# Decode attention over a 32,768-key cache: two more score columns on VectorE, a pipelined end, and longer rows for the output projection

## The chip, the cores and the metric

The kernel runs on one core of one Trainium2 chip. The metric is the device time of one execution in microseconds (us). PE is the matmul engine, VectorE (DVE) and ScalarE (ACT) the two elementwise engines, SP the engine that issues the loads, PEld PE's loading of weights. The granted clock is the share of PE's full speed that the trace records.

## The reference

One token attends over 32 heads of 32,768 keys of 192 numbers, then goes through a small two-layer network. All data is bf16. What matters here:

```python
q = (layernorm(x) @ wq).reshape(32, 192)             # x: 640, wq: 640 x 6144
p = softmax((q · k_cache) * 192**-0.5)               # k_cache: 32 x 32768 x 192, 403 MB
o = p · v_cache                                      # v_cache: the same size
h = x + o.reshape(6144) @ wo                         # wo: 6144 x 640
out = h + relu(layernorm(h) @ w1) @ w2               # w1: 640 x 1536, w2: 1536 x 640
```

K and V are read once and used for one query: 805 MB of the 825 MB that the kernel loads.

## The kernel before

A head's keys come in loads of 64 columns (8192 keys, 128 partitions x 24,576 B, 3 MiB), K and V alternately, from one queue into three buffers each. A load is worked in two chunks of 32 columns. Of a chunk, 12 columns are scored on VectorE (multiply by the query, reduce) and 20 on PE, which must first transpose them in 30 blocks of 128 x 128, copied out of PSUM by ScalarE. The exponentials, and their sums, are ScalarE's; then PE multiplies the probabilities with V. The last load of all is cut into 40, 16 and 8 columns.

```python
full = [(JL, [(J, 20), (J, 20)])] * (Sk // (P * JL))          # J = 32 columns, 20 of them on PE
ends = full[:-1] + [(40, [(20, 12), (20, 12)]), (16, [(16, 10)]), (8, [(8, 4)])]
# ... (cut)
wo_view = A_wo.rearrange("(b p) n -> p b n", p=P)             # rows of 1280 B
# ... (cut)
def o_scale(h):
    # ... (cut)
    nc.vector.tensor_scalar_mul(out=dst[:, 0, n0:n0 + Dh], in0=o[:, 0:Dh], scalar1=s[0:2, 1:2])
    nc.scalar.activation(out=dst[:, 1, n0:n0 + Dh], in_=o[:, Dh:2 * Dh], func=F.Copy, scale=s[0:2, 1:2])
# ... (cut)
for g in range(G):                      # chunks of all heads
    # ... loads of this chunk (cut)
    transposes(g)
    if g > 0:
        pv(g - 1)                       # probabilities times V, one chunk behind
    scores_pe(g)
    sc = scores_dve(g)
    # ... once per head: denominator, scaling, turning, projection, next query (cut)
    exp_dve(g, sc)
den_mm(H - 1); den_rec(H - 1); pv(G - 1); o_scale(H - 1); o_turn(H - 1); project(H // 2 - 1)
# ... second layernorm and the two layers (cut)
```

The softmax here doesn't subtract the row's maximum and nothing guards it: scores larger than these inputs give would overflow.

Of the kernel before, what the change touches and what calls it, by code (L numbers as in the profile page):

```python
# [9 lines left out]
F = mybir.ActivationFunctionType  # L10
# [3 lines left out]
def kernel(  # L14
# [12 lines left out]
    nc = tc.nc  # L27
    P = nc.NUM_PARTITIONS

    Bsz, Sq, D = A_x.shape  # L30
    _, H, Sk, Dh = A_k_cache.shape
# [9 lines left out]
    JL = 64  # L41
    J = 32
# [2 lines left out]



    full = [(JL, [(J, 20), (J, 20)])] * (Sk // (P * JL))
    ends = full[:-1] + [(40, [(20, 12), (20, 12)]), (16, [(16, 10)]), (8, [(8, 4)])]
    NEND = 3  # L50
    loads = []
    chunks = []
    for h in range(H):
        k0 = c = 0
# [8 lines left out]
            k0 += P * jl  # L63
        assert k0 == Sk
    G = len(chunks)
    NCH = [sum(1 for q in chunks if q[0] == h) for h in range(H)]
    NCM = max(NCH)
    NBM = max(q[5] for q in chunks) * Dh // P
# [3 lines left out]
    kpool = ctx.enter_context(tc.tile_pool(name="kpool", bufs=3))  # L72
    vpool = ctx.enter_context(tc.tile_pool(name="vpool", bufs=3))
# [3 lines left out]
    tsb = ctx.enter_context(tc.tile_pool(name="tsb", bufs=2))  # L77
    prp = ctx.enter_context(tc.tile_pool(name="prp", bufs=1))
    scp = ctx.enter_context(tc.tile_pool(name="scp", bufs=3))
    pcp = ctx.enter_context(tc.tile_pool(name="pcp", bufs=3))  # L80
    small = ctx.enter_context(tc.tile_pool(name="small", bufs=2))
    tps = ctx.enter_context(tc.tile_pool(name="tps", bufs=3, space=bass.MemoryType.PSUM))
    sps = ctx.enter_context(tc.tile_pool(name="sps", bufs=1, space=bass.MemoryType.PSUM))
# [4 lines left out]
    def mm_bank(shape, dtype, name):  # L88
        return mps.tile(shape, dtype, tag="mm", name=name)

    k_hd = A_k_cache.rearrange("b h s d -> (b h) s d")
    v_hd = A_v_cache.rearrange("b h s d -> (b h) s d")
    wq_view = A_wq.rearrange("(c p) n -> p c n", p=P)
    wo_view = A_wo.rearrange("(b p) n -> p b n", p=P)


    x_row = const.tile([DT, P], bf16)
# [5 lines left out]
    vt_t = {}  # L103
# [6 lines left out]

    def load_wo(pr):
        t = wop.tile([P, 3, D], bf16, name="wo")
        nc.sync.dma_start(out=t[:], in_=wo_view[:, 3 * pr:3 * pr + 3, :])
        wo_t[pr] = t

    def load_part(ld, src, pool, tag, name):
        h, k0, jl = loads[ld]
        if ld == len(loads) - 1:
            pool, tag, size = wqp, "wq", DT * QG * Dh
        else:  # L120
            size = JL * Dh
        t = pool.tile([P, size], bf16, tag=tag, name=name)
        nc.sync.dma_start(out=t[:, 0:jl * Dh], in_=src[h, k0:k0 + P * jl, :].rearrange("(p j) d -> p (j d)", p=P))
        return t

    def load_k(ld):
        kt_t[ld] = load_part(ld, k_hd, kpool, "kt", "kt")

    def load_v(ld):
        vt_t[ld] = load_part(ld, v_hd, vpool, "vt", "vt")  # L130

    w_t = {}

    def load_w(name, src, pool, tag, pieces):
        n, N = src.shape[0] // P, src.shape[1]
        assert n * N <= JL * Dh and n % pieces == 0
        t = pool.tile([P, JL * Dh], bf16, tag=tag, name=tag)
        v = t[:, 0:n * N].rearrange("p (c n) -> p c n", n=N)
        for i in range(pieces):
            c0, c1 = i * n // pieces, (i + 1) * n // pieces  # L140
            nc.sync.dma_start(out=v[:, c0:c1], in_=src.rearrange("(c p) n -> p c n", p=P)[:, c0:c1])
        for c in range(n):
            w_t[name, c] = v[:, c, :]
# [21 lines left out]
    o_pair = [const.tile([2, 2, 2 * Dh], f32, name=f"o_pair{i}") for i in range(2)]  # L165
# [25 lines left out]
    with tc.manual_schedule():  # L191
# [37 lines left out]
        def transposes(g):  # L229
            h, c, ld, c0, jc, jp = chunks[g]  # L230
            kt = kt_t[ld]
            NB = jp * Dh // P
            kT = tsb.tile([P, NBM, P], bf16, name="kT")
            for b0 in range(0, NB, 8):
                nb = min(8, NB - b0)
                tp = tps.tile([P, 8, P], bf16, name="tp")
                for b in range(nb):
                    off = (c0 + jc - jp) * Dh + (b0 + b) * P
                    nc.tensor.transpose(out=tp[:, b, :], in_=kt[:, off:off + P], identity=ident_b[:])  # L239
                nc.scalar.copy(out=kT[:, b0:b0 + nb, :], in_=tp[:, 0:nb, :])  # L240
            kT_t[g] = kT
# [18 lines left out]
        def scores_dve(g):  # L260
            h, c, ld, c0, jc, jp = chunks[g]
            kt = kt_t[ld]
            JD = jc - jp
            qb = qb_t[h]
            pr = prp.tile([P, JDM, Dh], f32, name="pr")
            nc.vector.tensor_tensor(out=pr[:, 0:JD, :], in0=kt[:, c0 * Dh:(c0 + JD) * Dh].rearrange("p (j d) -> p j d", d=Dh),  # L266
                                    in1=qb[:].unsqueeze(1).to_broadcast([P, JD, Dh]), op=A.mult)
            sc = scp.tile([P, J], f32, name="sc")
            nc.vector.reduce_sum(out=sc[:, 0:JD], in_=pr[:, 0:JD, :], axis=mybir.AxisListType.X)  # L269
            return sc  # L270

        def exp_dve(g, sc):
            h, c, ld, c0, jc, jp = chunks[g]
            JD = jc - jp
            pA = pcp.tile([P, J], bf16, name="pA")
            nc.scalar.activation(out=pA[:, 0:JD], in_=sc[:, 0:JD], func=F.Exp, scale=SCALE,  # L276
                                 accum_out=dsums[:, h, 2 * c:2 * c + 1])
            pA_t[g] = pA

        def pv(g):  # L280

            h, c, ld, c0, jc, jp = chunks[g]
            JD = jc - jp
            vt, pA, pB = vt_t[ld], pA_t.pop(g), pB_t.pop(g)
            if c == 0:
                o_t[h] = ops.tile([2, 2 * Dh], f32, name="o_ps")
            o = o_t[h]
            order = list(range(JD, jc, 2)) + list(range(0, JD, 2))
            for i, j in enumerate(order):
                p = pA[:, j:j + 2] if j < JD else pB[:, j - JD:j - JD + 2]  # L290
                first = c == 0 and i == 0
                last = c == NCH[h] - 1 and i == len(order) - 1
                nc.tensor.matmul(o[:], lhsT=p, rhs=vt[:, (c0 + j) * Dh:(c0 + j + 2) * Dh], start=first, stop=last)  # L293
# [3 lines left out]
        def den_mm(h):  # L297
            d = mm_bank([P, 2 * NCM], f32, "den")
            nc.tensor.matmul(d[:], lhsT=ones_mat[:], rhs=dsums[:, h, :], start=True, stop=True)  # L299
            den_t[h] = d  # L300

        def den_rec(h):
            d = den_t.pop(h)
            s = small.tile([P, 2], f32, tag="rec", name="rec")
            nc.vector.reduce_sum(out=s[:, 0:1], in_=d[:], axis=mybir.AxisListType.X)  # L305
            nc.vector.reciprocal(out=s[:, 1:2], in_=s[:, 0:1])
            den_t[h] = s

        def o_scale(h):
            s = den_t.pop(h)  # L310
            o = o_t.pop(h)
            dst = o_pair[(h // 2) % 2]
            n0 = (h % 2) * Dh
            nc.vector.tensor_scalar_mul(out=dst[:, 0, n0:n0 + Dh], in0=o[:, 0:Dh], scalar1=s[0:2, 1:2])  # L314
            nc.scalar.activation(out=dst[:, 1, n0:n0 + Dh], in_=o[:, Dh:2 * Dh], func=F.Copy, scale=s[0:2, 1:2])  # L315

        oT_t = {}

# [21 lines left out]

        load_k(0)
        load_v(0)
        q_rows(0)
        q_spread(0)
        for g in range(G):
            h, c, ld, c0, jc, jp = chunks[g]
            end = ld - (len(loads) - NEND)
            if end == 0 and c0 == 0:
                for i in range(NEND):
                    load_k(ld + i)  # L350
                for i in range(NEND):
                    load_v(ld + i)

                load_w("w1", B_w1, kpool, "kt", 1)
                load_w("w2", B_w2, vpool, "vt", 2)
            elif end < 0 and c0 == 0 and g > 0:
                load_k(ld)
                load_v(ld)
            if c == 1 and h % 2 == 0:
                load_wo(h // 2)  # L360
            if c == 3 and h % QG == QG - 2 and h + 2 < H:
                load_wq(h // QG + 1)
            transposes(g)
            if g > 0:
                pv(g - 1)
            scores_pe(g)
            sc = scores_dve(g)
            if c == 0 and h > 0:
                den_mm(h - 1)
                den_rec(h - 1)  # L370
                o_scale(h - 1)
            if c == 1 and h > 0:
                o_turn(h - 1)
            if c == 2 and h > 0 and h % 2 == 0:
                project(h // 2 - 1)
            if c == 4 and h + 1 < H:
                q_rows(h + 1)
            if c == 5 and h + 1 < H:
                q_spread(h + 1)
            exp_dve(g, sc)  # L380
        den_mm(H - 1)
        den_rec(H - 1)
        pv(G - 1)
        o_scale(H - 1)
        o_turn(H - 1)
        project(H // 2 - 1)
# [55 lines left out]
```

## Time and profile before

| | before |
|---|---|
| time | 1954.15 us |
| span in the profile, first to last instruction | 1952.3 us |
| DMA queue, share of 16 engines | 99.0% |
| busy: PE, VectorE, ScalarE | 82%, 69%, 55% |
| instruction packets (16,384 B) | 159 |
| last full K load landed | 1912.1 us |
| the output scaled | 28.6 us after that |
| end of the span | 11.6 us after the scaling |

The last three rows cut the run at two moments. "Landed" is the last of the sixteen counts on the load's semaphore, from the trace; "scaled" is the start of VectorE's scaling of the last head in the chain of waits. Up to the first moment the loads set the time; between the two, the compute of the last two chunks and of the four small ones; after the second, a serial tail of small steps.

### The profile page before, as it was taken

The numbers are of one execution on the slowest core, as the hardware profiler recorded it, in microseconds if no ns is written. First come the engines' busy times: TensorE is split into PE (matmuls) and PEld (weight loads), VectorE is DVE, ScalarE is ACT, GpSimd is POOL, SyncE is SP. The second block draws the span as 40 slices with busy tenths as digits, with TensorE's granted clock in tenths as the row PEclk, the third lists the DMA queues.
The fourth block names the chain that finished last, engine by engine and source line by source line (L and its number), as shares of the span: only waits on it lengthen the run. The fifth ranks groups of instructions, "written<-read, shape, count | busy, mean of one in ns | idle before, by whom it ended". The sixth has DMA issues, their size and how long they took to land.

```text
span 1952.3 us, 44906 instructions
## 1 busy us (share of the span) xinstructions
PE 1594.4 (82%) x20392; PEld 1122.4 (57%) x20392; DVE 1338.0 (69%) x654; ACT 1067.5 (55%) x2223; POOL 0.7 (0%) x6
## 2 busy tenths in 40 slices
PE   6887887878788788787888877888788887887887
PEld 4655565555556556555555655655555565565655
DVE  5766777667666676676767666777666766676675
ACT  4555555555555555555655555555555555555554
POOL 0000000000000000000000000000000000000000
PEclk9989889989998889998988989899899989898998
DMA  9999999999999999999999999999999999999996
GB/s 405 431 429 429 430 431 430 429 429 431 431 430 428 430 431 430 431 429 431 430 429 430 429 431 430 430 431 424 431 431 428 425 421 431 427 430 426 430 421 253
DMA packets 51522, 827.85 MB, mean 424 GB/s; under 512 B 4612, under 2 KB 17412, under 8 KB 18564
## 3 DMA queue, kind: packets, MB, share of 16 engines
q1 hardware_dynamic: 51332, 824.99, 99.0%
q8 instruction: 159, 2.61, 0.5%
q14 instruction: 31, 0.25, 0.0%
HBM read 824.97 MB, written 0.00 MB: 423 GB/s over the span
## 4 chain that ended last, share of the span: by engine, by line
DMA 77%; PE 17%; ACT 4%; DVE 1%; issue 1%; SPq 0%; ACTq 0%
DMA kt<-in_A_k_cache_dram 75%; PE o_ps L293 8%; PE tp L239 6%; ACT kT L240 3%; DMA vt<-in_A_v_cache_dram 1%; DVE pr L266 1%; PE sp L249 1%; PE sp L253 1%; PE sp L251 1%; PE qps L205 0%; ACT pA L276 0%; ACT pB L256 0%; DVE o_pair L314 0%; PE oT_ps L327 0%; ACT row_e L208 0%
## 5 line engine op out<-in xcount | busy, mean ns | idle before, releaser
L240 ACT COPY kT<-tp 128x1024 bf16<-128x1024 bf16 (+1 forms) x1025 | 905.2, 966 | 343.1 <-PE tp L239 340.2
L266 DVE TENSOR_TENSOR pr<-kt,qb 128x2304 f32<-128x2304 bf16 (+1 forms) x258 | 655.0, 2539 | 483.3 <-DMA kt<-in_A_k_cache_dram 479.9
L239 PE MATMUL tp<-ident_b,kt 128*128 128x128 bf16 x7677 | 599.3, 242 | 342.8 <-DMA kt<-in_A_k_cache_dram 269.7
L239 PEld LDWEIGHTS <-kt 128*128 128x128 bf16 x7677 | 531.1, 110 | 381.2 <-DMA kt<-in_A_k_cache_dram 280.2
L269 DVE TENSOR_REDUCE sc<-pr 128x12 f32<-128x2304 f32 (+1 forms) x258 | 654.3, 2536 | 27.6 <-ACT kT L240 1.4
L293 PE MATMUL o_ps<-vt,pB 128*2 128x384 bf16 x2559 | 498.8, 346 | 2.6 <-DMA vt<-in_A_v_cache_dram 2.6
L293 PEld LDWEIGHTS <-pB 128*2 128x2 bf16 x2559 | 203.8, 87 | 226.9 <-issue 65.9
L256 ACT ACTIVATE pB<-sp 128x20 bf16<-128x20 f32 (+1 forms) x258 | 48.4, 188 | 492.4 <-PE sp L253 492.4
L293 PE MATMUL o_ps<-vt,pA 128*2 128x384 bf16 x1537 | 291.9, 326 | 0.0
L249 PEld LDWEIGHTS <-kT 128*128 128x128 bf16 x2559 | 196.1, 96 | 85.7 <-issue 84.7
L249 PE MATMUL sp<-qm,kT 128*128 128x2 bf16 x2559 | 218.6, 164 | 0.5 <-ACT kT L240 0.5
L251 PE MATMUL sp<-qm,kT 128*128 128x1 bf16 x2559 | 215.0, 163 | 0.0
L253 PE MATMUL sp<-qm,kT 128*128 128x1 bf16 x2559 | 215.0, 163 | 0.0
L251 PEld LDWEIGHTS <-kT 128*128 128x128 bf16 x2559 | 198.7, 96 | 0.0
L293 PEld LDWEIGHTS <-pA 128*2 128x2 bf16 x1537 | 129.1, 84 | 120.8
L253 PEld LDWEIGHTS <-kT 128*128 128x128 bf16 x2559 | 197.4, 96 | 0.0
L276 ACT ACTIVATE pA<-sc 128x12 bf16<-128x12 f32 (+1 forms) x258 | 52.8, 205 | 0.0
L256 ACT ACTIVATION_READ_ACCUMULATOR pB<-sp 128x1 f32 x258 | 50.1, 194 | 0.0
L276 ACT ACTIVATION_READ_ACCUMULATOR pA<-sc 128x1 f32 x258 | 49.3, 191 | 0.0
L305 DVE TENSOR_REDUCE rec<-den 128x1 f32<-128x20 f32 x32 | 5.7, 179 | 60.2 <-PE den L299 60.2
L315 ACT ACTIVATE o_pair<-o_ps,rec 2x192 f32<-2x192 f32 x32 | 13.2, 412 | 26.9 <-DVE o_pair L314 26.9
L327 PE MATMUL oT_ps<-ident_f,o_pair 2*128 2x1 f32 x192 | 24.2, 247 | 0.1
(60 smaller groups left out, 191.4 us busy)
## 6 DMA issues: line engine op xcount, KB each, us to landing
kt<-in_A_k_cache_dram SPq DMA_DIRECT2D x127, 3072.0 KB, 35.7
vt<-in_A_v_cache_dram SPq DMA_DIRECT2D x127, 3072.0 KB, 31.4
wq<-in_A_wq_dram SPq DMA_DIRECT2D x8, 960.0 KB, 34.7
wo<-in_A_wo_dram SPq DMA_DIRECT2D x16, 480.0 KB, 31.2
kt<-in_A_k_cache_dram SPq DMA_DIRECT2D x1, 1920.0 KB, 30.7
vt<-in_A_v_cache_dram SPq DMA_DIRECT2D x1, 1920.0 KB, 25.4
kt<-in_B_w_dram SPq DMA_DIRECT2D x1, 1920.0 KB, 17.1
vt<-in_B_w_dram SPq DMA_DIRECT2D x2, 960.0 KB, 13.3
```

Source lines behind the costliest of these rows:

```text
L239: nc.tensor.transpose(out=tp[:, b, :], in_=kt[:, off:off + P], identity=ident_b[:])
L240: nc.scalar.copy(out=kT[:, b0:b0 + nb, :], in_=tp[:, 0:nb, :])
L249: nc.tensor.matmul(sp[:, 2 * i:2 * i + 2], lhsT=kT[:, 3 * i + 1, :], rhs=qm[:, 1:3], start=True, stop=False, skip_group_check=True)
L251: nc.tensor.matmul(sp[:, 2 * i:2 * i + 1], lhsT=kT[:, 3 * i, :], rhs=qm[:, 0:1], start=False, stop=False, skip_group_check=True)
L253: nc.tensor.matmul(sp[:, 2 * i + 1:2 * i + 2], lhsT=kT[:, 3 * i + 2, :], rhs=qm[:, 3:4], start=False, stop=True, skip_group_check=True)
L256: nc.scalar.activation(out=pB[:, 0:JP], in_=sp[:, 0:JP], func=F.Exp, scale=SCALE, accum_out=dsums[:, h, 2 * c + 1:2 * c + 2])
L266: nc.vector.tensor_tensor(out=pr[:, 0:JD, :], in0=kt[:, c0 * Dh:(c0 + JD) * Dh].rearrange("p (j d) -> p j d", d=Dh), in1=qb[:].unsqueeze(1 ...
L269: nc.vector.reduce_sum(out=sc[:, 0:JD], in_=pr[:, 0:JD, :], axis=mybir.AxisListType.X)
L276: nc.scalar.activation(out=pA[:, 0:JD], in_=sc[:, 0:JD], func=F.Exp, scale=SCALE, accum_out=dsums[:, h, 2 * c:2 * c + 1])
L293: nc.tensor.matmul(o[:], lhsT=p, rhs=vt[:, (c0 + j) * Dh:(c0 + j + 2) * Dh], start=first, stop=last)
L315: nc.scalar.activation(out=dst[:, 1, n0:n0 + Dh], in_=o[:, Dh:2 * Dh], func=F.Copy, scale=s[0:2, 1:2])
L327: nc.tensor.matmul(ps[:, b:b + 1], lhsT=src[:, i, b * P:(b + 1) * P], rhs=ident_f[0:2, i:i + 1], start=(i == 0), stop=(i == 1))
```

## The change

It moves work off PE (18 columns of a full chunk instead of 20, VectorE 14 instead of 12), lengthens the contiguous rows of wo from 1280 to 3840 B by giving each partition three neighbouring rows (the output is permuted to match when it is scaled), and reorders the last four chunks, so that PE transposes the next chunk before it scores this one. The V loads of the end come in four pieces instead of three. The core of the diff:

```diff
-    full = [(JL, [(J, 20), (J, 20)])] * (Sk // (P * JL))
+    full = [(JL, [(J, 18), (J, 18)])] * (Sk // (P * JL))
-    pcp = ctx.enter_context(tc.tile_pool(name="pcp", bufs=3))
+    pcp = ctx.enter_context(tc.tile_pool(name="pcp", bufs=6))
-    wo_view = A_wo.rearrange("(b p) n -> p b n", p=P)
+    wo_view = A_wo.rearrange("(g p b) n -> g p b n", p=P, b=3)
 ...
     def load_v(ld):
-        vt_t[ld] = load_part(ld, v_hd, vpool, "vt", "vt")
+        parts = [(q[3], q[3] + q[4]) for q in chunks if q[2] == ld] if ld >= len(loads) - NEND else None
+        vt_t[ld] = load_part(ld, v_hd, vpool, "vt", "vt", parts)
 ...
-            nc.vector.tensor_scalar_mul(out=dst[:, 0, n0:n0 + Dh], in0=o[:, 0:Dh], scalar1=s[0:2, 1:2])
-            nc.scalar.activation(out=dst[:, 1, n0:n0 + Dh], in_=o[:, Dh:2 * Dh], func=F.Copy, scale=s[0:2, 1:2])
+            dst = o_pair[(h // 2) % 2][:].rearrange("q i (b p) -> q i p b", b=3)
+            p0, p1 = (h % 2) * Dh // 3, (h % 2 + 1) * Dh // 3
+            src = o[:].rearrange("q (i p b) -> q i p b", i=2, b=3)
+            nc.vector.tensor_scalar_mul(out=dst[:, 0, p0:p1, :], in0=src[:, 0], scalar1=s[0:2, 1:2])
+            nc.scalar.activation(out=dst[:, 1, p0:p1, :], in_=src[:, 1], func=F.Copy, scale=s[0:2, 1:2])
 ... (the loads of the end and w1, w2 are issued here, in the same order as before)
+        transposes(ENDS[0])
+        pv(ENDS[0] - 1)
+        sc = scores_dve(ENDS[0])
+        for i, g in enumerate(ENDS[1:]):
+            transposes(g)
+            scores_pe(g - 1)
+            exp_dve(g - 1, sc)
+            sc = scores_dve(g)
+            if i > 0:
+                pv(g - 2)
+        scores_pe(G - 1)
+        exp_dve(G - 1, sc)
         den_mm(H - 1)
         den_rec(H - 1)
+        pv(G - 2)
         pv(G - 1)
```

More of the change, by code (lines that the diff above doesn't have):

```diff
@@ L65 @@
     G = len(chunks)
+    ENDS = [g for g in range(G) if chunks[g][2] >= len(loads) - NEND]
     NCH = [sum(1 for q in chunks if q[0] == h) for h in range(H)]
@@ L112, in load_wo, with load_part @@
         t = wop.tile([P, 3, D], bf16, name="wo")
-        nc.sync.dma_start(out=t[:], in_=wo_view[:, 3 * pr:3 * pr + 3, :])
+        nc.sync.dma_start(out=t[:], in_=wo_view[pr])
         wo_t[pr] = t
-    def load_part(ld, src, pool, tag, name):
+    def load_part(ld, src, pool, tag, name, parts=None):
         h, k0, jl = loads[ld]
@@ L122, in load_part @@
         t = pool.tile([P, size], bf16, tag=tag, name=name)
-        nc.sync.dma_start(out=t[:, 0:jl * Dh], in_=src[h, k0:k0 + P * jl, :].rearrange("(p j) d -> p (j d)", p=P))
+        rows = src[h, k0:k0 + P * jl, :].rearrange("(p j) d -> p (j d)", p=P)
+        for j0, j1 in parts or [(0, jl)]:
+            nc.sync.dma_start(out=t[:, j0 * Dh:j1 * Dh], in_=rows[:, j0 * Dh:j1 * Dh])
         return t
@@ L311, in o_scale @@
             o = o_t.pop(h)
-            dst = o_pair[(h // 2) % 2]
-            n0 = (h % 2) * Dh
-            nc.vector.tensor_scalar_mul(out=dst[:, 0, n0:n0 + Dh], in0=o[:, 0:Dh], scalar1=s[0:2, 1:2])
-            nc.scalar.activation(out=dst[:, 1, n0:n0 + Dh], in_=o[:, Dh:2 * Dh], func=F.Copy, scale=s[0:2, 1:2])
+            dst = o_pair[(h // 2) % 2][:].rearrange("q i (b p) -> q i p b", b=3)
[3 more added lines that the diff above has]
+            nc.scalar.activation(out=dst[:, 1, p0:p1, :], in_=src[:, 1], func=F.Copy, scale=s[0:2, 1:2])
         oT_t = {}
@@ L344 @@
         q_spread(0)
-        for g in range(G):
+        for g in range(ENDS[0]):
             h, c, ld, c0, jc, jp = chunks[g]
-            end = ld - (len(loads) - NEND)
-            if end == 0 and c0 == 0:
-                for i in range(NEND):
-                    load_k(ld + i)
-                for i in range(NEND):
-                    load_v(ld + i)
-                load_w("w1", B_w1, kpool, "kt", 1)
-                load_w("w2", B_w2, vpool, "vt", 2)
-            elif end < 0 and c0 == 0 and g > 0:
+            if c0 == 0 and g > 0:
                 load_k(ld)
@@ L380 @@
             exp_dve(g, sc)
+        for ld in range(len(loads) - NEND, len(loads)):
+            load_k(ld)
+        for ld in range(len(loads) - NEND, len(loads)):
+            load_v(ld)
+        load_w("w1", B_w1, kpool, "kt", 1)
+        load_w("w2", B_w2, vpool, "vt", 2)
+        transposes(ENDS[0])
[10 more added lines that the diff above has]
+        exp_dve(G - 1, sc)
         den_mm(H - 1)
         den_rec(H - 1)
+        pv(G - 2)
         pv(G - 1)
```

## The prediction

> **What bounds the kernel now.** I read the page's queue lines first, then the chain of work that ended last, then the busy times of the engines in short stretches of the end, then the DMA packets and landings that the trace records.
>
> ```profile
> DMA  9999999999999999999999999999999999999996
> GB/s 405 431 429 429 430 431 430 429 429 431 431 430 428 430 431 430 431 429 431 430 429 430 429 431 430 430 431 424 431 431 428 425 421 431 427 430 426 430 421 253
> q1 hardware_dynamic: 51332, 824.99, 99.0%
> q8 instruction: 159, 2.61, 0.5%
> DMA 77%; PE 17%; ACT 4%; DVE 1%; issue 1%; SPq 0%; ACTq 0%
> ```
>
> The 16 DMA engines are busy 99% of the span at about 430 GB/s, and only the last slice (48.8 us) falls to 253. The chain is mostly the K loads. K and V alone are 805 MB and neither kernel can avoid them: the time is the queue plus what follows it.
>
> The compute engines have room in the middle. One load of 64 columns comes every 15.07 us (K landings at 13.6 and 1912.1 us, 126 loads apart). VectorE's groups, shapes kept apart (busy us, mean ns | idle before, releaser):
>
> ```profile
> L266 DVE TENSOR_TENSOR pr<-kt,qb 128x2304 f32<-128x2304 bf16 x254 | 649.2, 2556 | 481.6 <-DMA kt<-in_A_k_cache_dram 478.3
> L269 DVE TENSOR_REDUCE sc<-pr 128x12 f32<-128x2304 f32 x254 | 648.5, 2553 | 27.2 <-ACT kT L240 1.4
> ```
>
> Two chunks of 2.56 + 2.55 us make 10.2 us of VectorE in 15.07, and its idle time is a wait for K. PE is busy 82% of the span.
>
> The end, in stretches (PE, PEld, DVE, ACT, POOL busy; PE clock; DMA share; GB/s):
>
> ```profile
> 1900.00:1905.00 5.00, 4.74 (x74) 3.42 (x72) 4.96 (x2) 3.37 (x8) 0.00 (x0) 1.00 0.83 350
> 1915.00:1920.00 5.00, 5.00 (x56) 2.74 (x55) 4.94 (x2) 1.88 (x5) 0.00 (x0) 0.78 0.47 199
> 1938.00:1940.00 2.00, 1.46 (x15) 0.78 (x14) 0.06 (x1) 0.61 (x5) 0.00 (x0) 1.00 0.58 211
> 1944.00:1946.00 2.00, 0.64 (x21) 0.57 (x21) 0.83 (x4) 0.29 (x1) 0.00 (x0) 0.62 0.00 0
> ```
>
> The DMA share falls to a half while loads are still outstanding. It looks like starvation by buffers, but the trace's landings say otherwise. A load's semaphore is counted up 16 times. For the last full K load the first eight counts come from 1890.3 to 1894.6 us, the last eight from 1910.3 to 1912.1. **Eight engines are some 16 us ahead of the other eight**, and the load is usable only when the late eight are done. At 13 us all sixteen came within 0.6 us, so the lag grows over the run. The packets from 1915 to 1920 us show eight in flight throughout: the late eight never run dry before the last weight lands at 1944.0. The early eight do, which costs nothing.
>
> Why late? The 159 instruction packets (16,384 B, mean 930 ns) are 148 us of engine time. In the last 45 us, wherever I can tell (near 1903, 1917, 1927), such a packet takes a place from the late eight. All 159 on eight engines is 18.5 us each, near the observed lag (the early eight lose 1 to 3 us at some stalled issues). So I take the late eight as the bound: data, plus instruction fetches, plus what follows.
>
> [...] median 55 ns for 1280 B, 121 for 3072 B, 912 for 24,576 B, a line of 0.0368 ns per byte plus 8 ns. [...]
>
> **The change, part by part.**
>
> *14 columns on VectorE.* For 250 chunks VectorE goes from 12 to 14 columns: 5.11 x 14/12 = 5.96 us a chunk, 11.9 a load, still under 15.07. PE loses 3 of 30 transposes and 3 of 30 score matmuls a chunk. ScalarE keeps four copies a chunk, the last 384 wide rather than 768. All this lies beside the loads, so worth **0 in the middle**. But PE's program shrinks from 40,315 to 37,267 instructions (counted in the compiled programs): 3048/256 = 12 fetches fewer, 12 x 0.93 us / 8 late engines = **-1.4 us**. If the fetches were on all sixteen it would be -0.7.
>
> *wo rows of 3840 B.* 16 loads of 480 KB go from 6144 packets to 2048. Per engine 384 x 55 ns = 21.1 us becomes 128 x (8 + 0.0368 x 3840 = 149 ns) = 19.1 us: **-2.1 us** on the path. The permuted rows are undone where the output of a head is scaled (strided writes of 2x192 elements, 0.41 us now); no added instruction, **0**.
>
> *Values in four pieces.* The 40-column V load becomes two; 8 packets more per engine x 8 ns = **+0.1 us**. Its first half lands about 2 us sooner.
>
> *End pipelined.* Everything on the late engines comes 3.4 us sooner: last full K at 1908.7 (before 1912.1), the 40-column K at 1920.7 (1924.1), its V at 1925.9 and 1928.1 (1931.5), the last V at 1931.0 (1934.4), w2 at 1940.6 (1944.0). Before, from the last full K to the scaling of the output took 1912.1 to 1940.7 = 28.6 us, PE busy nearly all of it:
>
> ```profile
> 1931.52 0.04 issue
> 1931.56 1.78 PE o_ps L293 x10
> ...
> 1939.51 0.40 PE den L299 x2
> 1939.91 0.75 PE o_ps L293 x4
> 1940.68 0.42 DVE o_pair L314
> ```
>
> Now, by durations of these instructions: VectorE from 1908.7 two chunks of 5.96 to 1920.7, then the four end chunks, unchanged and back to back (1924.2 to 1936.4 before = 12.2 us), to 1932.9. PE from 1908.7: transposes 3.0, values 3.6, scores 0.6, transposes 1.9, values 2.7, scores 0.6 = 1921.2; first end transposes 1.2, values 2.7 = 1925.1; second transposes 1.2, scores 0.5, third transposes 1.0 = 1927.8; then alternating with ScalarE's copies (2.2 and 1.8 us): scores, values (1.6), transposes (0.4), scores, values (1.6), last scores at about 1932.8. VectorE and PE meet. Then exponentials 0.5, denominator 0.4, values of the last two chunks 1.3 + 0.75: 1935.8, 27.1 us after the K load. That is **-1.5 us** beside the 3.4. It is small because putting the third chunk's values behind the denominator costs 1.3 us of what the lookahead wins.
>
> The rest, scaling to the end of the span (1940.7 to 1952.3 = 11.6 us), stays. w2 would be wanted at 1935.8 + 6.8 = 1942.6, lands at 1940.6: no new wait. Sum: -1.4 - 2.1 + 0.1 - 1.5 = **-4.9 us**, 1954.15 to **1949.3 us**.
>
> **Rivals.** (1) *The columns pay in full:* if PE set the pace, a tenth fewer transposes and scores of PE's 1594 us would save some 100 us. Against: VectorE waits 480 us and PE 270 us for K. It would show as faster by over 2%; I hold it impossible while 825 MB cross at 430 GB/s. (2) *VectorE becomes the bound:* it does at the end only. There each full chunk is 0.85 us longer, 1.7 us over the last load; if the values or copies wait for it, the 1.5 us of the end vanish: 1950.8. (3) *The end starves on buffers:* if the queue were really empty, the earlier issues would bring 5 us or more, 1945. For it: 199 GB/s in 1915 to 1920. Against: eight packets in flight then. (4) *DMA gain hidden or smaller:* fetches on all engines and packet overhead overlapped: only the end's gain and 1 us, 1951.7. (5) *PE at half clock at the end* (it was 0.5 after idle stretches): transposes 112 ns rather than 63 would cost 1 to 2 us.
>
> **Range and chances.** The steady part is fixed to about 1 us (three runs within 0.02 us), the end's order to about 2 us. So 1949.3 us, 8 in 10 between 1947.0 and 1951.8. A change of 2% would be 39 us; the whole end after the last full K is 40 us, and no engine has a way to lose 39: faster 0.01, same 0.985, slower 0.005.
>
> **What would show it.** GB/s of the full slices still 429 to 431; instruction packets about 147; wo packets 2048 of 3840 B near 150 ns; last full K landing near 1908.7, with the halves still some 14 us apart; VectorE's products near 2.98 us; the output scaled 27 us after that landing; 11.6 us from there to the end. Wrong if the last full K lands outside 1907.5 to 1910.5, or if PE waits for V, ScalarE's copies or VectorE's exponentials by more than 1 us in the last 15 us before the scaling.

Two passages are cut from this text. What stands between the cuts are median durations of the load packets in the trace of the kernel before, by size, and the line through them, from which the 8 ns for each packet are estimated. Of other figures in the text, these stand in the traces:

- **256 instructions for each fetch:** the page of the kernel before lists 20,392 matmuls and as many weight loads on PE, with 159 instruction packets, 256.5 for each; that of the changed kernel 18,868 and as many, with 147 packets, 256.7.
- **A load is usable when the late eight are done:** the sixteenth count of the last full K load came at 1912.1 us; PE began on it at 1912.12 and VectorE at 1912.17.
- **0.5 after idle stretches:** PE waited 3.4 us for that load, and the clock record shows 0.50 from 1910.4 to 1917.2.
- **Transposes of 112 and 63 ns:** thirty of them from 1912.1 took 3.38 us at that clock, and twenty-four from 1889.9 took 1.50 us at the full one.

## The result

The changed kernel takes **1949.53 us** (1949.33 to 1949.98, four runs), 4.6 us less than the 1954.15 before. The ratio of the fast runs is 0.9976, 95% interval 0.9959 to 0.9994. A ratio is always the mean time of one kernel's fast runs over the mean of the other's in the same rounds, so it is not quite the ratio of the medians.

The same lines of the page as the prediction showed, now of the changed kernel: the queue first, then the share of the last chain by engine, then VectorE's two groups (busy us, mean ns, idle before):

```profile
DMA  9999999999999999999999999999999999999996
q1 hardware_dynamic: 47380, 824.99, 99.1%
q8 instruction: 147, 2.41, 0.4%
DMA 77%; DVE 14%; PE 8%; ACT 1%; issue 0%; SPq 0%; DVEq 0%; ACTq 0%
```

```profile
L270 DVE TENSOR_TENSOR pr<-kt,qb 128x2688 f32<-128x2688 bf16 x254 | 750.7, 2956 | 308.3 <-DMA kt<-in_A_k_cache_dram 304.8
L273 DVE TENSOR_REDUCE sc<-pr 128x14 f32<-128x2688 f32 x254 | 750.1, 2953 | 27.2 <-ACT kT L244 1.4
```

The queue is as full as before, with 4096 packets fewer for wo and 12 instruction packets fewer. VectorE still waits 305 us for K, so it is not the bound in the middle. The chain that ended last now runs through DVE at 14% where it ran through PE at 17%. These shares are of the whole span (14% is 273 us, the end some 40), so they say little of the end; the next lines do.

The chain of waits at the end (start us, us, what), after the last full K load:

```profile
1907.83 2.97 DVE pr L270
...
1919.92 1.77 DVE pr L270
...
1931.14 0.96 DVE sc L273
1932.10 0.02 issue
1932.12 0.31 ACT pA L280 x2
1932.43 0.04 issue
1932.47 0.40 PE den L303 x2
1932.87 2.05 PE o_ps L297 x12
1934.93 0.03 issue
1934.95 0.54 DVE o_pair L320
1935.52 0.59 ACT o_pair L321
1936.11 0.04 issue
1936.15 1.28 PE oT_ps L333 x10
```

From 1907.8 to 1932.1 it is VectorE's products and sums back to back, with no wait between them (the dots stand for more of the same): VectorE, not PE, now sets the end. Then exponentials, denominator, the last twelve value matmuls and the scaling at 1934.95. So the three parts of the run are:

| | last full K landed | from there to the scaling | from the scaling to the end | span |
|---|---|---|---|---|
| before | 1912.1 | 28.6 | 11.6 | 1952.3 |
| predicted | 1908.7 | 27.1 | 11.6 | 1947.4 |
| changed | 1907.7 | 27.2 | 12.7 | 1947.6 |

The total was met, but read at these two moments two of its terms are each a microsecond off, in opposite directions. The experiments below take them apart.

### The profile page after: what moved, and what is told of

It is laid out like the page before. It is cut to its first block, busy times and chain, and to the rows that moved or that the text cites. A ratio compares the mean times of both kernels' runs of the same rounds, so it can differ in the third digit from the quotient of the medians.

```text
span 1947.6 us, 41859 instructions
## 1 busy us (share of the span) xinstructions
PE 1552.9 (80%) x18868; PEld 1065.8 (55%) x18868; DVE 1543.0 (79%) x654; ACT 996.2 (51%) x2223; POOL 0.7 (0%) x6
## 3 DMA queue, kind: packets, MB, share of 16 engines
q1 hardware_dynamic: 47380, 824.99, 99.1%
## 4 chain that ended last, share of the span: by engine, by line
DMA 77%; DVE 14%; PE 8%; ACT 1%; issue 0%; SPq 0%; DVEq 0%; ACTq 0%
DMA kt<-in_A_k_cache_dram 77%; DVE pr L270 9%; DVE sc L273 4%; PE o_ps L297 4%; PE tp L243 3%; ACT kT L244 1%; PE sp L253 0%; DVE o_pair L320 0%; PE sp L257 0%; PE sp L255 0%; PE qps L209 0%; PE den L303 0%; ACT row_e L212 0%; DVE rec L309 0%; PE yps L419 0%
## 5 line engine op out<-in xcount | busy, mean ns | idle before, releaser
L270 DVE TENSOR_TENSOR pr<-kt,qb 128x2688 f32<-128x2688 bf16 (+1 forms) x258 | 756.6, 2932 | 308.4 <-DMA kt<-in_A_k_cache_dram 304.8
L244 ACT COPY kT<-tp 128x1024 bf16<-128x1024 bf16 (+1 forms) x1025 | 822.9, 885 | 331.0 <-PE tp L243 329.7
L243 PE MATMUL tp<-ident_b,kt 128*128 128x128 bf16 x6915 | 556.8, 245 | 380.7 <-DMA kt<-in_A_k_cache_dram 294.9
L273 DVE TENSOR_REDUCE sc<-pr 128x14 f32<-128x2688 f32 (+1 forms) x258 | 755.9, 2930 | 27.6 <-ACT kT L244 1.4
L243 PEld LDWEIGHTS <-kt 128*128 128x128 bf16 x6915 | 488.0, 112 | 419.1 <-DMA kt<-in_A_k_cache_dram 305.7
L297 PE MATMUL o_ps<-vt,pA 128*2 128x384 bf16 x1791 | 333.8, 326 | 0.0
L260 ACT ACTIVATE pB<-sp 128x18 bf16<-128x18 f32 (+1 forms) x258 | 48.4, 187 | 521.6 <-PE sp L257 521.5
L253 PEld LDWEIGHTS <-kT 128*128 128x128 bf16 x2305 | 177.1, 96 | 84.8 <-issue 84.1
L255 PE MATMUL sp<-qm,kT 128*128 128x1 bf16 x2305 | 195.9, 163 | 0.0
L257 PE MATMUL sp<-qm,kT 128*128 128x1 bf16 x2305 | 195.9, 163 | 0.0
L255 PEld LDWEIGHTS <-kT 128*128 128x128 bf16 x2305 | 179.6, 96 | 0.0
L257 PEld LDWEIGHTS <-kT 128*128 128x128 bf16 x2305 | 178.4, 96 | 0.0
L280 ACT ACTIVATE pA<-sc 128x14 bf16<-128x14 f32 (+1 forms) x258 | 54.7, 212 | 43.0 <-DVE sc L273 42.2
```

The source lines that it names most:

```text
L243: nc.tensor.transpose(out=tp[:, b, :], in_=kt[:, off:off + P], identity=ident_b[:])
L244: nc.scalar.copy(out=kT[:, b0:b0 + nb, :], in_=tp[:, 0:nb, :])
L253: nc.tensor.matmul(sp[:, 2 * i:2 * i + 2], lhsT=kT[:, 3 * i + 1, :], rhs=qm[:, 1:3], start=True, stop=False, skip_group_check=True)
L255: nc.tensor.matmul(sp[:, 2 * i:2 * i + 1], lhsT=kT[:, 3 * i, :], rhs=qm[:, 0:1], start=False, stop=False, skip_group_check=True)
L257: nc.tensor.matmul(sp[:, 2 * i + 1:2 * i + 2], lhsT=kT[:, 3 * i + 2, :], rhs=qm[:, 3:4], start=False, stop=True, skip_group_check=True)
L260: nc.scalar.activation(out=pB[:, 0:JP], in_=sp[:, 0:JP], func=F.Exp, scale=SCALE, accum_out=dsums[:, h, 2 * c + 1:2 * c + 2])
```

## The experiments

Each experiment was compared with runs of the kernel before on the same chip. The table has the three parts of every profiled run (one profile each); the times are medians of four runs, of five where the text says so. The landing of the last full K load repeats well: the four variants that have the same middle as the changed kernel (changed, end_order, end_fixed, v_in_one) show 1907.7 to 1907.9, and the two with the middle of the kernel before (before, end_only) 1912.1 and 1911.7. It is one load of many, though, and the last of its counts moves in steps of some 1.4 us (four counts of the 11th load of the kernel before come by 165.2 and the next at 166.5; more under columns_only). Where a gain is small, the mean of the late eight counts is given too.

The profiles differ in one more thing. Around PE's wait for the last full K load its clock is granted at a half, for 6.8 us in before, columns_only and end_order and for 3.4 us in wo_rows_only, end_only, v_in_one, changed and end_fixed. Differences of a microsecond in "to the scaling" between single profiles can come from that; the medians have to bear them out.

| run | time us | ratio to before | last full K landed | to the scaling | to the end |
|---|---|---|---|---|---|
| changed | 1949.53 | 0.9976 | 1907.7 | 27.2 | 12.7 |
| wo_rows_only | 1954.62 | 1.0001 | 1911.4 | 28.7 | 13.0 |
| columns_only | 1953.69 | 0.9995 | 1909.1 | 31.5 | 11.7 |
| end_only | 1953.06 | 0.9992 | 1911.7 | 27.5 | 11.7 |
| v_in_one | 1950.88 | 0.9979 | 1907.7 | 29.7 | 12.5 |
| end_order | 1949.51 | 0.9972 | 1907.8 | 27.5 | 13.1 |
| end_fixed | 1949.86 | 0.9977 | 1907.9 | 27.2 | 12.9 |
| columns_16_end_fixed | 1948.19 | 0.9968 | 1906.3 | 27.2 | 12.9 |
| pe_fetch | 1957.83 | 1.0017 | 1915.7 | 28.1 | 12.4 |
| pe_fetch_tiny | 1957.05 | 1.0014 | 1915.5 | 27.2 | 12.4 |
| k_two_runs | 1968.98 | 1.0074 | 1927.2 | 27.9 | 12.5 |
| wo_eight_engines | 1977.86 | 1.0121 | 1937.7 | 27.7 | 12.5 |
| pool_fetch | 3482.34 | 1.7816 | 1922.2 | not read | not read |

### Each part alone

**wo_rows_only**: the kernel before with only the change of `wo_view` and of the scaling.

> The kernel before with only the wo rows of 3840 B and the strided scaling. My theory (the late eight DMA engines set the pace, 256 fewer packets on each at 8 ns of overhead): the last full K lands 2.1 us sooner than in the kernel before (1912.1), but the trace of the changed kernel shows that the scaling of a head now takes 0.53 + 0.58 us rather than 0.41 + 0.42 and that the span from the scaling to the end grew by 1.0 us, so about 1953.0 us (1952.2 to 1953.4). Rival (packet overhead hidden): the landing stays at 1912.1 and the strided end costs up to 1 us: 1954.2 to 1955.2. 159 instruction packets either way.

The landing moved by 0.7 us against the kernel before (0.8 as the mean of the late eight), less than the 2.1 expected, and the end after the scaling lasted 13.0 us instead of 11.6. Time: 1954.62 beside 1954.49, ratio 1.0001, interval 0.9986 to 1.0016. **Alone the longer rows bring nothing that these runs can tell**: the packets win less than a microsecond, and the profile gives more than that back after the scaling. The expected 1953.0 was missed.

**columns_only**: the kernel before with only `(J, 20)` turned into `(J, 18)`.

> The kernel before with only 14 columns of each full chunk on VectorE (18 on PE). My theory: 12 instruction packets fewer (147), on the late eight engines, so the last full K lands 1.4 us sooner (1910.7); after it PE, which sets the old end, has 12 transposes and 12 score matmuls fewer, about 1 us: 1951.7 us (1950.9 to 1952.6). If the fetches are spread over all sixteen engines: landing 0.7 us sooner, 1952.4. Rival (fetches hidden, columns cost or win only at the end): landing at 1912.1, 1953.1. Rival (PE sets the pace in the middle): over 50 us faster.

The landing came 3.0 us sooner, twice what was expected, and yet the run gained only 0.8 us (1953.69 beside 1954.49; the interval includes 1). What was won before the last K load was lost after it: 31.5 us to the scaling instead of 28.6. In the lists of waits from 1905 to 1942 us (engine, line, waited for: us in total, times, longest), the same wait stands in the kernel before (first line, with its load in the chain of waits) and here (last line):

```profile
PE o_ps L293 <- DMA vt<-in_A_v_cache_dram: 0.8, 1, 0.8
1906.10 25.42 DMA vt<-in_A_v_cache_dram
```

```profile
PE o_ps L293 <- DMA vt<-in_A_v_cache_dram: 3.0, 1, 3.0
```

The stretches after it in columns_only (PE, PEld, DVE, ACT, POOL busy; clock; DMA share; GB/s):

```profile
1928.00:1930.00 2.00, 0.00 (x0) 0.00 (x0) 1.97 (x2) 0.89 (x2) 0.00 (x0) 1.00 0.98 372
1930.00:1932.00 2.00, 1.89 (x9) 0.91 (x9) 1.86 (x3) 0.00 (x0) 0.00 (x0) 0.73 0.66 260
1932.00:1934.00 2.00, 2.00 (x30) 1.37 (x28) 1.43 (x2) 0.46 (x4) 0.00 (x0) 0.50 0.67 218
```

PE, with less to transpose, arrives at the values of the 40-column load before its V has landed (1930.1 us) and waits 3.0 us. During 1928 to 1930 it does nothing at all. After the wait its clock is granted at a half (0.50 in 1932 to 1934), and the fifteen transposes that follow take 1.42 us in the chain, where they took 0.86 in the kernel before. So a wait of 0.8 us grew to 3.0 in place of the work removed. The 2.9 us lost are of two parts: 1.6 us, because this V landed only 1.4 us sooner than before (1930.1 against 1931.5) where the last full K landed 3.0 sooner, and 1.3 us from the V's landing to the scaling, which the slower clock accounts for (the transposes above, and 2.60 us for the ten value matmuls before them instead of 1.78).

The 3.0 us at the last full K load are not typical. Of the 30 K loads from the 101st on, 21 had their last count 1.2 to 1.6 us sooner, and 9, the last full one among them, 2.8 to 3.0, a step more. As the mean of the late eight counts the gain at the last full K load is 2.1 us.

**end_only**: the kernel before with only the new end (order of the last chunks, V in four pieces, six buffers).

> The kernel before with only the end: transposes one chunk ahead of the scores, V in four pieces, six buffers for the probabilities. My theory: the last full K lands as before (1912.1 to 1912.3), 159 instruction packets, and the scaling of the output comes 27 to 27.5 us after it instead of 28.6: 1952.6 to 1953.2 us. Rival (the end starves on buffers and V in pieces feeds it sooner): 1950 us or less.

27.5 us to the scaling instead of 28.6, 1953.06 us beside 1954.49: a gain of 1.4 us, where 1.0 to 1.5 was expected. The interval of the ratio (0.9975 to 1.0009) includes 1, but each of its four runs (1952.69 to 1953.34) is faster than each of the seven of the kernel before beside it (1954.04 to 1955.51). The rival, that pieces of V would feed a starving end and bring 4 us or more, did not come about.

The three parts alone change the medians by +0.1, -0.8 and -1.4 us, a sum of -2.1. Together they change it by -4.6. The missing 2.5 us are about the 2.9 us that the columns lost in the old end and do not lose in the new one. That reading is argued: the columns were not run with the new end alone, and the four runs of columns_only spread from 1952.4 to 1955.7.

**v_in_one**: the changed kernel with the 40-column V load in one piece again (`parts = None`), five rounds.

> The changed kernel with the 40-column V load in one piece again. In columns_only PE waited 3.0 us for it in the old end (landing 1930.1) and then ran its transposes at 100 ns rather than 57. In the changed kernel the first values are wanted at 1927.2 and the whole load lands at 1928.2: PE waits 1.0 us, about 0.7 of it beyond VectorE's chain. If the pieces matter for this: 0.5 to 1.5 us slower than the changed kernel, 1950.0 to 1951.0. If the lookahead alone carries the end: 1949.5.

(The 100 and 57 ns are estimates; the chains give 1.42 and 0.86 us for the fifteen transposes, 95 and 57 ns each.)

The median is 1950.88, 1.35 us above the changed kernel's; its runs spread from 1950.2 to 1952.1 and its kernel before ran 1954.76, so by the ratios (0.9979 and 0.9976) the difference is only half a microsecond, well inside their intervals. The profiled run shows where its time went all the same: the scaling came 29.7 us after the K load instead of 27.2. PE's clock and work, first in v_in_one, then in the changed kernel, in the same stretches:

```profile
1926.00:1928.00 2.00, 1.04 (x25) 1.00 (x25) 1.97 (x2) 2.00 (x8) 0.00 (x0) 0.96 1.01 393
1928.00:1930.00 2.00, 1.40 (x5) 0.59 (x5) 1.86 (x3) 0.91 (x5) 0.00 (x0) 0.50 0.62 245
1930.00:1932.00 2.00, 2.00 (x15) 0.91 (x13) 1.89 (x2) 0.00 (x0) 0.00 (x0) 0.69 0.66 203
```

```profile
1926.00:1928.00 2.00, 1.74 (x30) 1.34 (x30) 1.97 (x2) 2.00 (x8) 0.00 (x0) 1.00 0.98 382
1928.00:1930.00 2.00, 2.00 (x30) 1.28 (x28) 1.90 (x2) 1.37 (x6) 0.00 (x0) 1.00 0.68 270
1930.00:1932.00 2.00, 1.75 (x16) 0.80 (x13) 1.86 (x3) 0.91 (x7) 0.00 (x0) 1.00 0.70 211
```

With V in one piece PE waited 1.3 us for it (landing 1928.6), the clock fell to 0.50, and the ten value matmuls took 3.07 us in the chain; in the changed kernel they ran from 1927.2 to 1929.0. So the wait is 1.3 us, and the slow clock after it about as much again. PE had short idle stretches of 0.2 and 0.3 us before this wait, and the half clock began at 1927.8, 0.5 us into the wait of 1.3 us: there were 1.0 us of idle time in the 3.4 us before (3.41 us is the shortest clock record in the traces of the kernel before and of the changed one). Why the median lost less than the profiled run is not shown: I have no profile of the others.

### What sets the landing

**pe_fetch**: the changed kernel with twenty matmuls a chunk that nobody reads.

```diff
+            for _ in range(20 if h < H - 1 else 0):
+                nc.tensor.matmul(sp[:, 30:32], lhsT=kT[:, 0, :], rhs=qm[:, 1:3],
+                                 start=True, stop=True, skip_group_check=True)
```

> The changed kernel with 20 more tiny matmuls a chunk on PE (writing columns of the score bank that nothing reads), in all heads but the last: 9920 more PE instructions, 39 more instruction packets (186). They are 0.6 us of PE a chunk, PE stays under one load's period. My theory (each packet of 0.93 us stands in the queue of one of the late eight engines): 39 x 0.93 / 8 = +4.5 us, last full K at 1912.2, and the halves of its landing 17 to 18 us apart instead of 13. If the fetches are spread over all sixteen engines: +2.3 us, the halves 13 apart. If fetches are hidden: 0 us.

8.3 us slower than the changed kernel by the medians, 8.0 at the landing: nearly twice the 4.5 expected, and nowhere near the rivals' 0 and 2.3. The expected 0.6 us of PE a chunk was an estimate; by the page of the next run, pe_fetch_tiny, it is 0.45 for that run's matmuls (PE busy 1665.2 us instead of 1552.9, over 248 chunks). But these matmuls read weights from SBUF too, so the same was tried without that.

**pe_fetch_tiny**: the same count, one element by one element (`sp[0:1, 30:31]` from `ones_row[0:1, 0:1]` twice).

> As pe_fetch (20 more matmuls a chunk in all heads but the last, 39 more instruction packets), but of one element by one element, so that they read next to nothing from SBUF and load no weights of 128 x 128. If the fetches cost what pe_fetch showed (1.6 us of a late engine each, 39/8 each): about +8 us over the changed kernel, last full K at 1915 to 1916, 1957 to 1958 us. If pe_fetch was slow by its reads of SBUF and not by its fetches: nearer to the changed kernel, below 1952 us.

7.5 us slower, landing at 1915.5 beside 1915.7. **It is the fetching, not the work.** The instruction packets, in the page's line of that queue:

```profile
q8 instruction: 186, 3.05, 0.6%
```

The sixteen counts of one K load in the middle (the 61st), in us, sorted, from the traces' records of landings (eight, then eight):

```
changed        905.0 905.1 905.2 905.2 905.4 906.1 908.4 911.3 | 916.3 916.5 916.5 916.6 917.7 918.0 918.1 918.2
pe_fetch_tiny  905.0 905.0 905.1 905.2 905.3 906.0 908.3 910.3 | 919.3 920.6 920.7 920.8 920.8 920.8 921.0 921.0
```

The early eight are where they were, within a microsecond. Only the late eight moved, by 3 to 4 us. So up to this load the added instruction fetches had delayed those eight engines and no others. (By the last full K load the first counts are later too, 1894.4 against 1887.4. There the load itself was issued 7.7 us later, 1880.9 against 1873.1. A load is issued when a buffer is free, and that waits for the late engines: in the chain of the changed kernel an earlier K load lands at 1863.98, VectorE reads it in products until 1873.10, and the issue follows at 1873.12.) At the last full K load it is 7.8 us for 39 packets over eight engines (4.9 each): **1.6 us of an engine for each fetch**, where the prediction took the packet's own 0.93 us. The means of the late eight agree: 7.5 us for these, and 2.1 for the fetches that columns_only saves (11 by that moment, 1.4 an engine), 1.5 us each. Why a fetch costs more than its packet lasts, no run shows. In early loads the late engines lie apart in steps: at the 11th load of the kernel before, eight counts come from 163.4 to 165.0, four from 165.0 to 165.2 and four from 166.5 to 166.8. These steps of some 1.4 us, too, are longer than a packet.

**pool_fetch**: 9920 tiny instructions on GpSimd instead (multiplying one element by 1).

> The changed kernel with 9920 tiny instructions on GpSimd, which has nothing else to do: 39 more instruction packets, no more work for PE. If it is the fetching and not PE's work that costs, and GpSimd's fetches stand on the same eight engines as PE's: +4.5 us; on other engines: 0 (if on the early eight, whose slack is 13 us) to +2.3 us; if fetches are hidden: 0.

A miss. GpSimd needed 3481 us for the 9920 instructions, 0.35 us each, so the time says nothing. Nor did they come as 16 KB packets: that count stayed at 147, and 78 more packets of 8192 B appeared in another queue. The first count of the last full K load came 13.9 us later and the last 14.5, early and late engines alike, with packets of K and V of 920.7 ns on average instead of 915.5. The question it was made for was answered by pe_fetch_tiny.

**wo_eight_engines**: five of the sixteen wo loads written with 8 as the slowest dimension of the source.

```diff
+            nc.sync.dma_start(out=t[:].rearrange("p b n -> p (b n)"),
+                              in_=A_wo.rearrange("(g y x b) n -> g x y (b n)", y=16, x=8, b=3)[pr])
```

> The changed kernel with 5 of the 16 wo loads (pairs 1, 4, 7, 10, 13) read so that the slowest dimension of the source is 8, with rows permuted once more and undone at the scaling (8 instructions instead of one, in the middle of the run). If that confines such a load to eight engines, each of these gets 5 x 1.2 = 6 us more and the others 6 us less. My theory (eight engines set the pace): about 6 us faster if the eight named are the early ones (last full K at 1901.7, halves about 1 us apart), 6 us slower if they are the late ones (halves 25 apart). Rivals (the engines level out, or the end starves on buffers): within 0.5 us of the changed kernel. If all sixteen still carry it: no difference, and its landings count up sixteen times.

28 us slower than the changed kernel. The trace shows these five loads on eight engines: their semaphores were stepped once some 1.1 us after the issue and then by eight landings. But, by the landings of these loads, the eight engines are four of the early and four others, and the cost was not 1.2 us per load. At the last full K load fourteen engines landed between 1919.9 and 1923.8, and **two at 1937.5 and 1937.7**, 30 us later than in the changed kernel, 6 us for each of the five loads. The wo packets took 177 ns on average instead of 150. Why two engines suffered so much more is left open. What the run does show is that fourteen of sixteen engines were done 14 us sooner, and the time followed the two.

**k_two_runs**: each full K row of 24,576 B in two runs of 12,288 B, with a small gap between them in SBUF.

> The changed kernel with each full K load's row of 24,576 B written as two runs of 12,288 B (16 elements of gap in SBUF): 16,256 more packets, 1016 more on each DMA engine, all else equal. It measures what a packet costs. If the 8 ns of the durations are on the path (the term -2.1 us of the prediction): 1016 x 8 ns = +8 us, 1957.6 us, and a median near 460 ns for the new packets. If they overlap: less, down to 0. wo_rows_only (landing 0.7 us sooner for 256 packets fewer) would point to 3 ns, +3 us.

19.4 us slower than the changed kernel; landing 19.5 us later for 1016 more packets on each engine, so **19 ns a packet**, where the durations alone (465.5 ns twice against 918.4 ns for V's rows in the same run) give 12.6, and the prediction's line 8. All sixteen engines moved alike (the first count of the 61st K load from 905.0 to 913.1, the last from 918.2 to 927.6). This does not fit the wo rows, where 256 packets fewer on each engine brought 0.7 us alone, and 0.9 to 1.9 with the columns (changed against columns_only from the 111th K load on; the new end's smaller loads are in that too): 3 ns a packet alone, 4 to 7 so. The price of a packet is not one number here, and what it depends on stays open. The gap also places the second half of each row 32 B off in SBUF; whether that has a share in the 19 ns was not tested.

### The end

**end_order**: the values of the last chunk but one ahead of the denominator (`pv(G - 2)` moved up two lines).

> The changed kernel with the values of the last chunk but one ahead of the denominator's matmuls. My theory: PE has 0.75 us of idle time before the denominator, so the denominator ends some 0.6 us later but only four matmuls follow it: the scaling 0.7 us sooner, 1948.8 us. If VectorE's reciprocal or anything else ends the wait: no change.

The median shows no gain, 1949.51, but it stands between two pairs: 1948.67 and 1948.84, where 1948.8 was expected, and 1950.18 and 1950.22. The profiled run is one of the slow pair. In it PE is 1.0 us behind already before the lines that were changed: its clock stayed at a half for longer after the wait for the last full K load, 6.8 us instead of 3.4. The stretch 1911 to 1913, first in the changed kernel, then here:

```profile
1911.00:1913.00 2.00, 2.00 (x13) 0.94 (x11) 2.00 (x1) 0.92 (x2) 0.00 (x0) 0.88 0.71 304
```

```profile
1911.00:1913.00 2.00, 2.00 (x7) 0.76 (x6) 2.00 (x1) 1.17 (x2) 0.00 (x0) 0.50 0.55 235
```

The nine value matmuls in it took 2.83 us instead of 2.06. PE then set the end instead of VectorE, its idle time was gone, and the moved matmuls pushed the denominator back to 1934.2 from 1932.5. So PE's place in the end varies by about a microsecond with the moment at which the clock rises. That the two fast runs met a faster clock is my reading; they have no profile. The experiment is inconclusive.

**end_fixed**: the permutation undone in the turning matmuls instead, whose weight rows are then read with a stride of three elements, two tiles for the halves, matmuls ordered by half; five rounds.

> The changed kernel with the permutation undone where the turned columns are read (stride of three elements in the weight load) instead of by strided writes of the scaling, the two halves of the output in two tiles, and the turning matmuls ordered by half. The traces say that the scaling on VectorE (0.54) and ScalarE (0.59 us) run one after the other and that 10 of the 12 turning matmuls follow both; here each scaling takes 0.41, they may run together, and half of the turning matmuls runs beside the second: 1.0 to 1.5 us less, 1948.3 us. If strided weight loads cost as much as strided writes: no gain.

No gain: 1949.86, ratio 0.9977. The scaling is back at 0.41 us, but the turning matmuls are slower (duration in ns min/median/max, then first and last start), first before, then here:

```profile
L327 PE MATMUL oT_ps<-ident_f,o_pair x12: 245/245/266, 1940.6 to 1942.2; 2*128 2x1 f32 x12
```

```profile
L332 PE MATMUL oT_ps<-ident_f,o_pair x12: 306/308/332, 1935.6 to 1937.5; 2*128 2x1 f32 x12
```

From the scaling to the last of them it is 2.7 us here, 2.5 in the changed kernel and 1.7 before. In the kernel before, six of these twelve matmuls ran before and during the scaling (four of them needed only the head before; the chain shows six after it, of 0.84 us); with the permuted rows every block needs both heads, and ten or twelve follow the scaling (1.28 us and 2.26 us). **The permutation costs the end about a microsecond wherever it is undone.**

**columns_16_end_fixed**: end_fixed with 16 columns on VectorE, 14 in the last full load; five rounds.

> end_fixed with 16 columns of each full chunk on VectorE, except in the last full load, which keeps 14 (one buffer instead of two for the scaled outputs, to make room): PE has 3000 instructions fewer, 12 instruction packets fewer (135). By what pe_fetch and columns_only showed (1.4 to 2 us per fetch on each late engine, 1.5 fetches fewer each): the last full K lands 2 to 3 us sooner, 1945.5 to 1946.5 us. VectorE needs 13.6 us of each load's 15; if it is late for the last loads or holds the K buffers too long, the gain is lost.

1948.19 us (1947.81 to 1948.66), ratio 0.9968 against 0.9977 of end_fixed in the same rounds. **This is the fastest of all**, by 1.3 us against the changed kernel. 135 instruction packets, landing at 1906.3, 1.6 us sooner than in end_fixed, somewhat less than the 2 to 3 expected (2.2 as the mean of the late eight). The price is visible in the page: VectorE is busy 89% of the span, and ScalarE waits 245 us in all for VectorE's sums. Little is left to move.

## Why the prediction was right

**The bound: right, and shown.** It took the late eight DMA engines as the bound. The added fetches, at the 61st load, delayed only them, by 3 to 4 us, and the time followed with 7.5 us (pe_fetch_tiny); two late engines, 14 us behind the other fourteen, made the run 28 us longer (wo_eight_engines). Rival 1, the columns paying in full, and rival 2, VectorE as the bound in the middle, are refuted by the queue at 99.1% and by VectorE's 305 us of waits for K. Rival 3, starvation at the end, would have needed more than end_only's 1.4 us. Rival 4, a smaller gain from the packets, is right of the wo rows alone. Rival 5, the half clock, is there in every profile named above; in the changed kernel it lasted 3.4 us after the last full K load and cost nothing that shows, since VectorE set the end.

**The landings, -3.4 us: right at most loads.** The last counts, in us:

| | before | columns_only | predicted | changed |
|---|---|---|---|---|
| last full K | 1912.1 | 1909.1 | 1908.7 | 1907.7 |
| K of 40 columns | 1924.1 | 1921.3 | 1920.7 | 1919.5 |
| its V, last piece | 1931.5 | 1930.1 | 1928.1 | 1928.2 |
| last V | 1934.4 | 1932.8 | 1931.0 | 1931.0 |
| w2 | 1944.0 | 1942.5 | 1940.6 | 1940.7 |

The forecast was met to 0.1 us but for the two K loads, which came 1.0 and 1.2 us sooner. VectorE began at the first of these, so that microsecond counted. It repeats in end_order, end_fixed and v_in_one, but it is a step of the last count at these loads, which a division by eight does not see: the mean of the late eight at the last full K load is 3.6 us sooner. Its two terms were less good than their sum:

**"12 x 0.93 us / 8 late engines = -1.4 us": right mechanism, too small.** As the mean of the late eight columns_only brought 2.1 us at the last full K load, since a fetch cost 1.5 to 1.6 us and not 0.93. The last count showed 3.0 there and 1.4 to 1.6 at most other loads. (The prediction's "250 chunks" are 254; its count of instructions is right.)

**"-2.1 us" for the wo rows: too large.** 0.6 to 1.0 us alone, 0.9 to 1.9 with the columns, over the K loads from the 111th on. The packets' durations were as forecast (149 ns), 2048 of them. The durations therefore overstate what 256 packets fewer save on an engine here; k_two_runs shows that elsewhere they understate it.

**"no added instruction, 0" for the permutation: wrong.** The scaling grew from 0.41 + 0.42 to 0.53 + 0.58 us, and the turning matmuls that used to run ahead of it now follow it. "From the scaling to the end, 11.6 us, stays" became 12.7. The step counted instructions and not what each had been waiting for. Of the 1.1 us, 0.2 is another thing: the two matmuls of the second layernorm took 0.57 us instead of 0.37 in this profile, and 0.37 in that of pe_fetch_tiny, whose tail is 12.4 us.

**"27.1 us after the K load": right**, 27.2. The list of durations, engine by engine, held: VectorE's sums ended at 1932.1 where 1932.9 was forecast with a landing 1.0 us later. "VectorE and PE meet" was nearly so: in the profiled run VectorE is in the chain, and end_order shows that PE takes its place when its half clock lasts 6.8 us instead of 3.4 and it falls 1.0 us behind. "PE busy nearly all of it" missed that the kernel before already waited 0.8 us for V, a wait that was about to grow. The step did not see that the columns and the end depend on each other: without the pieces of V and the lookahead, the columns' gain is lost to a wait for V and to the half clock after it. By its own sign of being wrong, PE waiting more than 1 us in the last 15 us before the scaling, the prediction is a close case: PE waited 0.5 us for copies and 0.7 for the last exponentials, none of them over 1 us, 1.2 in sum.

So -4.9 was forecast and -4.6 came (-4.7 in the profiled span), as the sum of -4.4 at the landing (forecast -3.4), -1.4 to the scaling (-1.5) and +1.1 after it (0). Part of the agreement is luck: the microsecond by which the last full K load came early and the 1.1 us of the tail cancelled, and inside the loads so did fetches that were worth more than forecast and packets that were worth less.

## What to carry to other kernels

When a load spreads over many DMA engines, look at the spread of its counts and not only at the mean busy share. Here the time followed the slowest engines: two of them at 1937.5 and 1937.7, 14 us behind the rest, made wo_eight_engines 28 us longer. And the queue that looked half empty at the end (a DMA share of 0.47 from 1915 to 1920 us in the kernel before) was that of engines that had run ahead: of the last full K load the first eight counts came by 1894.6 and the last eight from 1910.3. With the loads at 99% of the queue, fewer instructions were worth more than the work they do: 39 fetches added cost 7.5 us in pe_fetch_tiny, 1.6 us of an engine each. Cost a change of layout by what each consumer could start before it, and test parts of a change in pairs: here the columns gained 0.8 us alone, and 2.5 us of the gain came only with the parts together.
